# Attention with a token mixer: 128 of 8192 score columns per phase go from ScalarE's exponential to a polynomial on GpSimd and VectorE, with three instead of four buffers for raw weight blocks

## The chip, the cores and the metric

The kernel runs on one NeuronCore of a Trainium2 chip. Its five engines each work through a list of instructions in order and wait for each other on semaphores: TensorE (PE, with its weight loads as PEld), VectorE (DVE), ScalarE (ACT), GpSimd (POOL) and SyncE (SP), which here issues nearly all DMA transfers. The metric is the time of one launch on the device in microseconds (us), lower is better.

## The reference

Two branches work on the same x (2048 tokens, 512 channels, float32) and are mixed row by row with a gate: softmax attention with 32 heads of 16 channels, and a token mixer, that is a layer norm and a two-layer MLP across the 2048 tokens.

```python
g = sigmoid((x * gate_w).sum(-1, keepdims=True))
q, k, v = (x @ wqkv) as 32 heads of 16
a = softmax(q @ k.T * 16**-0.5) @ v @ wo          # per head, 2048 x 2048 scores
b = (w2 . gelu(w1 . layernorm(x).T + b1) + b2).T  # along the tokens, 1792 hidden
out = g * a + (1 - g) * b
```

Everything is wanted in nearly full float32, so the matrix products of the mixer are made in three parts (a high and a low part of each operand, without low times low).

## The kernel before

**The stages.** From 0 to about 123 us the kernel transposes x and makes v, q and k; from 123 to 275 us it makes the first layer of the mixer. The rest, 275 to about 1230 us, is the attention, in 128 *phases* (the loop over `p`, lines 993 to 1156), four to a *group*. A group is two heads and half of the queries. In one phase PE makes 16 score blocks of 128 keys by 512 queries (line 1067), something takes the exponential of each, and PE multiplies them by v in 64 small matmuls (line 963). The second layer of the mixer and the output projections have no time of their own: their matmuls (line 1076, tile `dn`) run beside the score matmuls, on the other half of PE's rows, 12 or 14 in a phase.

**Who makes the exponentials.** The blocks of a phase are numbered 0 to 15. Six of them (`SINGLE`, tile `p`) ACT reads from PSUM one by one, four (`TWO`) in two pairs of 1024 columns (line 1031). The last six (`EVAC` = 1, 3, 5, 8, 14, 15) DVE copies from PSUM to one SBUF tile `pe` of 3072 columns (line 1089); when all six are there ACT makes one exponential of the whole tile in place (line 1102). In ACT's list that big one stands at the end of the phase, behind the six and the two pairs. The results of `pe` are used one phase later: `HELD` lists the three pairs of copied blocks whose product with v heads the next phase's 64 matmuls.

**Order of the work.** The whole attention runs under a manual schedule: each engine's list is the order in which the Python code calls it. At the start of a phase with `ph == 0` the code asks for the next group's q stack (`load_q`, 8 transfers, line 470, tile `qs`); then for each even phase it builds the 14 matmul steps of the mixer that two phases share, and that building calls `load_weight` whenever a step begins a new block of four weight tiles (`fc % 4 == 0`, `second_layer`). After that, still with `ph == 0`, the previous group's result is stored (lines 949 and 951, tiles `ot`, 8 transfers). At `ph == 1` the code asks for the next group's k stack (`load_k`, 6 transfers, line 470, tile `ks`). All of these are on SP's one list. In the last phase of a group (`ph == 3`) matmuls 8 to 21 of the 64 each wait for one of those 14 transfers (`await_loads` in `apply_v`), and the scores of the next group read them.

**The weight blocks.** A block of `w2` (up to four 128x128 tiles) is brought to a raw tile by `load_weight` (line 146, `w_raw`, four buffers), split into a high part by a copy (`w_hi`, line 67) and a low part by a subtraction on GpSimd (`w_lo`, line 68), and is then in the list `ready`. In the attention `split_weight` is called only in the second of two phases (odd `p`), behind everything else of that phase, and only until `ready` holds two blocks. A row tile t of the second layer takes four blocks: two are asked for at the start of its first two phases, one in each of the next two pairs. Between the rows of t = 0 to 7 a late q projection takes one more pair of phases, so those rows start every 8 phases, and later ones every 6.

**GpSimd** has little to do in the attention: `w_lo`, a clearing of the sum tile once a group (line 999), and once a phase a one-element write (`token`, line 1080) that waits for the phase's last `dn` matmul and for which the next phase's first `dn` matmul waits.

Of the kernel before, what the change touches and what calls it, by code (L numbers as in the profile page):

```python
# [9 lines left out]
F32 = mybir.dt.float32  # L10
F32R = mybir.dt.float32r
BF16 = mybir.dt.bfloat16
I32 = mybir.dt.int32
AF = mybir.ActivationFunctionType
ALU = mybir.AluOpType
# [8 lines left out]
P = 128  # L24
# [4 lines left out]
DH = 16  # L29
# [3 lines left out]
NB = 512  # L33
NQ = S // NB
VC = DH + 1
SCALE = DH**-0.5
# [19 lines left out]

LEAST_SUM = 1e-35


@with_exitstack  # L60
def gated_mix(ctx: ExitStack, tc: tile.TileContext, a_x, a_wqkv, a_wo, b_w1, b_b1, b_w2, b_b2, gate_w, out):
    nc = tc.nc
# [15 lines left out]
    const = ctx.enter_context(tc.tile_pool(name="const", bufs=1))  # L78
# [18 lines left out]
    mv = const.tile([P, NS, 2], F32, name="mv")  # L97
    rs = const.tile([P, NS], F32, name="rs")

    const.tile([P, 16], F32, name="pad")  # L100
    upper = ctx.enter_context(tc.tile_pool(name="upper", bufs=1, side="right"))
    upper.tile([P, 56], F32, name="pad_upper")
    v_pool = ctx.enter_context(tc.tile_pool(name="v", bufs=1, reuse_waits="tile"))
# [11 lines left out]
    wk = wk_ctx.enter_context(tc.tile_pool(name="wk", bufs=3, side="right"))  # L115
# [19 lines left out]
    def load_weight():  # L135
        if blocks:
            src = blocks.pop(0)
            raw = wk.tile([P, NB], F32, name="w_raw", bufs=4)
            if len(src.shape) == 2:
                raw = raw[:, : src.shape[1]]  # L140
                dst = raw
            else:
                raw = raw[:, : src.shape[1] * P]
                dst = raw.rearrange("p (k s) -> p k s", s=P)
            with tc.issue_after(x_load.ins):
                nc.sync.dma_start(dst, src)
            loaded.append(raw)
# [30 lines left out]
    with tc.tile_pool(name="vp", bufs=1, side="right") as pool:  # L178
# [143 lines left out]
        y, t, w = (pool.tile([P, NS], F32, name=n) for n in "ytw")  # L322
# [103 lines left out]
    with tc.tile_pool(name="gl", bufs=2, side="right") as gl:  # L426
# [74 lines left out]
        for f0, cs in order.items():  # L501
            n = min(NB, F - f0) // P
# [79 lines left out]
    LAST = NG * PHASES - 1  # L582
# [163 lines left out]
    def invert(half, k, pairs, at):  # L746


        n = pairs * 2
        w = QW // DH  # L750
        t = out_pool.tile([P, w], F32, name="inv")[: n * DH]
        nc.sync.dma_start(t, r_d[half][k][:n].rearrange("r (a b) -> (r a) b", b=w))

        def turn():
            nc.vector.tensor_scalar_max(t, t, LEAST_SUM)
            nc.vector.reciprocal(t, t)

        def put_back():
            nc.sync.dma_start(ri_d[half][k][:n].rearrange("r (a b) -> (r a) b", b=w), t)

        if half and k == ND - 1:
            amid[at + 1] = [(turn,)]
            on_dve(at + 1, put_back)
        else:
            on_dve(at, turn)
            calls.setdefault(at + 1, []).insert(0, (put_back,))
# [110 lines left out]
    for t in range(NS):  # L877
        at = put(second_layer(t), at, [14] * 3)
        if queries:
            b, n = queries.pop(0)  # L880
# [32 lines left out]
    call(p0 + 9, fetch_o, 2, p0 + 13, p0 + 14, p0 + 14)  # L913
    call(LAST, lambda: fetch_o(3, LAST, LAST, LAST, pairs=3))

    token, mark = (out_pool.tile([1, 1], F32, name=name, bufs=1) for name in ("token", "mark"))

    EVAC = 1, 3, 5, 8, 14, 15
    SINGLE = 0, 2, 4, 6, 7, 9
    TWO = (10, 11), (12, 13)  # L920
    TURNS = [(0, 2), (4, 6), (7, 9), *TWO]
    HELD = [(1, 3), (5, 8), (14, 15)]

    def shares(n):

        for one in range(0, BANKS, 2):
            lows = [k for k in range(one)][::2] + [k for k in range(one + 1, BANKS)][::2]
            for third in lows:
                if n in (third, third + 1):
                    first, second = (low for low in lows if low != third)  # L930
                    return [first, first + 1, one, second, second + 1, 2 * third + 1 - n, n]


    def regions():
        return tc.tile_pool(name="ps_s", bufs=1, space=PSUM, reuse_waits="tile")
# [52 lines left out]

    engines = {getattr(mybir.EngineType, name) for name in ("PE", "Activation", "DVE", "Pool", "SP")}
    with tc.manual_schedule(engines=engines):  # L990
        held, fence, turn, spare = [], None, 0, 0
        landed.clear()

        for p in range(LAST + 1):
# [38 lines left out]
                    units[j] = *units[j][:3], pt[:, k - low, :]  # L1033

            pairs_done = []
            evac = evp.tile([P, len(EVAC), NB], F32, name="pe")
            units = {}
            share = shares(spare)
            pool = regions()
# [2 lines left out]
            for n in in_turn:  # L1042
                i, qb = head[n], qbs[n]
                c = at[i][qb]
                at[i][qb] += 1
                if n < TWO[0][0]:
                    if n >= BANKS:
                        ones[share[n - BANKS]] = psum.tile([P, NB], F32, name=f"s{share[n - BANKS]}")
                    s = ones[share[n % BANKS]]
                else:  # L1050
                    if n == TWO[0][0]:
                        pool.__exit__(None, None, None)
                        pool = regions()
                        psum = pool.__enter__()
                        twos = {}
                        for low in range(BANKS):
                            if low == share[2]:
                                av = psum.tile([P, NB], F32, name="av")
                            elif low in (share[0], share[1]):
                                twos[low] = psum.tile([P, NB], F32, name=f"u{low}")  # L1060
                            elif low not in twos:
                                two = psum.tile([P, 2, NB], F32, name=f"t{low}")
                                twos[low], twos[low + 1] = two[:, 0, :], two[:, 1, :]
                                twos[low, low + 1] = two
                    s = twos[share[(n - BANKS) % BANKS]]
                rows_i = slice(i * HALF, i * HALF + ROWS)
                nc.tensor.matmul(  # L1067
                    s,
                    kt[grp][rows_i, c * P : (c + 1) * P],
                    qt[grp][rows_i, qb * NB : (qb + 1) * NB],  # L1070
                    start=True,
                    stop=True,
                )
                if n < n_b:
                    ps, a, b, begin, last, done = beside[n]
                    mm = nc.tensor.matmul(ps, a[half], b[half], start=begin and not second, stop=last and bool(second))  # L1076
                    if n == 0 and fence is not None:
                        tc.add_manual_dep(mm.ins, fence.ins.name, SYNC, reason=REASON)
                    if n == n_b - 1:
                        fence = nc.gpsimd.memset(token, 0.0)  # L1080
                        tc.add_manual_dep(fence.ins, mm.ins.name, SYNC, reason=REASON)
                if n == in_turn[-2]:
                    if n_b and second and beside[-1][-1] in between:
                        between[beside[-1][-1]]()
                    for what, *args in amid.get(p, ()):
                        what(*args)
                if n in EVAC:
                    pt = evac[:, EVAC.index(n), :]
                    nc.vector.tensor_copy(pt, s)  # L1089
                    units[n] = i, c, qb, pt  # L1090
                elif n in SINGLE:
                    pt = ptp.tile([P, NB], F32, name="p1", bufs=len(SINGLE))
                    one = nc.scalar.activation(pt, s, AF.Exp, scale=SCALE)  # L1093
                    if n == SINGLE[-1] and p:
                        tc.add_manual_dep(one.ins, earlier.ins.name, SYNC, reason=EARLY)
                    units[n] = i, c, qb, pt
                else:
                    units[n] = i, c, qb, None
                    if n in (TWO[0][1], TWO[1][1]):
                        exps(n)  # L1100
            for x in ([evac] if p < LAST else [evac[:, :2, :], evac[:, 2:, :]]):
                done = nc.scalar.activation(x, x, AF.Exp, scale=SCALE)  # L1102
            tc.add_manual_dep(done.ins, pairs_done[0].ins.name, SYNC, reason=EARLY)
            evac_done.append(done)
# [206 lines left out]
```

## Time and profile before

| | |
|---|---|
| median of three runs | 1262.76 us (1262.38 to 1263.31) |
| the profiled execution | 1262.86 us, with a span of 1261.1 us from its first to its last instruction |
| granted TensorE clock over the span | 1.000 |
| busy share of the span | PE 99%, ACT 85%, DVE 67%, POOL 16% |
| the attention, from the first phase's scores to the last's | 275.5 to 1222.6 us |
| DMA traffic | 152.31 MB, 121 GB/s on average |

The page of the profile gives the busy time of each engine, the chain of work that ended last, and groups of equal instructions with their count, busy time and mean duration, followed by the idle time in front of them and who ended it. The timeline lists instructions in order of time: start, duration from the start of the first to the end of the last, engine, line, operation, tiles, count, and in brackets the idle time before. Matmuls overlap each other, so PE reads as busy while it is held up for short times. Instructions of ACT and DVE overlap too, by a start before the end of the one in front; what an engine gets done is read from the distance of ends or of starts, not from durations. GpSimd's durations are rough. SPq is SP's own queue: a transfer's row shows when it was issued, not when it landed.

### The profile page before, as it was taken

Reading aid. Unit: us, or ns where it says so; the run is one execution under the profiler, and the core shown is the slowest. Engines: PE = TensorE matmul, PEld = TensorE weight load, DVE = VectorE, ACT = ScalarE, POOL = GpSimd, SP = SyncE. Lnnn points to the kernel's source line nnn. Section 1 sums busy time; section 2 is a strip of 40 time slices with the busy share of each in tenths; the row PEclk is TensorE's granted clock in tenths of the full one; section 3 lists DMA queues with packets and bytes.
Section 4 is the critical chain, followed back from the end, with each engine's and each line's share of the span. In section 5 each row is a group of like instructions: output and inputs, shape, how many; then the busy total and the mean of one; then the engine's idle time right before and its main releaser. Section 6 shows DMA issues by size and latency. Waiting matters only on the chain.

```text
span 1261.1 us, 32707 instructions
## 1 busy us (share of the span) xinstructions
PE 1253.0 (99%) x13342; PEld 827.9 (66%) x13342; DVE 850.8 (67%) x1562; ACT 1068.7 (85%) x1405; POOL 199.2 (16%) x316
## 2 busy tenths in 40 slices
PE   9999999999999999999999999999999999999998
PEld 7888888875666666666666666666666666666656
DVE  5675453178767676667667677776777677678883
ACT  4453343269999999999999999999999999999990
POOL 0220444561011101010110101111111111000000
PEclk9999999999999999999999999999999999999999
DMA  4799443253754443534344433444543443367621
GB/s 130 249 341 330 146 124 108 80 139 109 207 126 102 88 100 83 160 84 97 85 100 94 105 87 79 93 86 81 116 99 77 86 100 60 56 165 174 152 61 70
DMA packets 100555, 152.31 MB, mean 121 GB/s; under 512 B 17109, under 2 KB 56171, under 8 KB 96300
## 3 DMA queue, kind: packets, MB, share of 16 engines
q1 hardware_dynamic: 99820, 149.08, 46.6%
q8 instruction: 107, 1.75, 0.6%
q10 hardware_dynamic: 576, 1.05, 0.2%
q14 instruction: 52, 0.43, 0.1%
HBM read 105.39 MB, written 44.68 MB: 119 GB/s over the span
## 4 chain that ended last, share of the span: by engine, by line
PE 99%; ACT 1%; DVE 0%; issue 0%
PE av L963 32%; PE s L1067 23%; PE acc L424 12%; PE t L1067 9%; PE acc L75 8%; PE t L963 5%; PE u L1067 3%; PE dn L1076 3%; PE pa L1162 2%; PE acc L199 1%; PE acc L268 1%; PE acc L245 0%; ACT p L1093 0%; ACT pe L1102 0%; PE dn L1162 0%; PE pa L1192 0%
## 5 line engine op out<-in xcount | busy, mean ns | idle before, releaser
L1093 ACT ACTIVATE p<-s 128x512 f32<-128x512 f32 x768 | 412.3, 790 | 0.1
L1102 ACT ACTIVATE pe<-pe 128x3072 f32<-128x3072 f32 x129 | 381.8, 2962 | 0.0
L1067 PE MATMUL s<-qs,ks 64*128 64x512 f32 x1280 | 330.0, 400 | 0.6 <-ACT p L1093 0.6
L1089 DVE COPY pe<-s 128x512 f32<-128x512 f32 x512 | 318.1, 683 | 4.8 <-PE s L1067 0.8
L1067 PEld LDWEIGHTS s<-qs,ks 64*128 64x128 f32 x1280 | 225.6, 184 | 95.4 <-issue 45.3
L1031 ACT ACTIVATE p<-t 128x1024 f32<-128x1024 f32 x256 | 278.4, 1265 | 0.0
L963 PE MATMUL av<-p,v 128*32 128x256 f32 x3880 | 227.2, 379 | 0.0
L1089 DVE COPY pe<-u 128x512 f32<-128x512 f32 x256 | 164.8, 686 | 72.1 <-PE u L1067 72.1
L963 PE MATMUL av<-pe,v 128*32 128x256 f32 x3072 | 192.5, 383 | 0.0
L985 DVE TENSOR_TENSOR ot<-av,ot 128x512 f32<-128x512 f32 (+2 forms) x160 | 93.1, 582 | 141.5 <-PE av L963 140.2
L68 POOL TENSOR_TENSOR w_lo<-w_raw,w_hi 128x512 fp32r<-128x512 f32 (+1 forms) x128 | 153.5, 1206 | 194.5 <-ACT w_hi L67 101.8
L1076 PE MATMUL dn<-u_lo,w_hi 64*128 64x512 f32 x448 | 180.8, 404 | 0.0
L1076 PE MATMUL dn<-u_hi,w_hi 64*128 64x512 f32 x448 | 180.7, 403 | 0.0
L963 PEld LDWEIGHTS av<-p,v 128*32 128x32 f32 x3880 | 126.1, 110 | 83.2 <-ACT p L1093 0.2
L1076 PE MATMUL dn<-u_hi,w_lo 64*128 64x512 f32 x448 | 180.7, 403 | 0.0
L1067 PE MATMUL t<-qs,ks 64*128 64x512 f32 x512 | 142.5, 413 | 0.0
L963 PEld LDWEIGHTS av<-pe,v 128*32 128x32 f32 x3072 | 86.8, 109 | 82.1 <-ACT p L1093 37.8
L1080 POOL MEMSET token<- 1x1 f32 x128 | 11.3, 88 | 742.4 <-PE dn L1076 720.5
L67 ACT CAST w_hi<-w_raw 128x512 fp32r<-128x512 f32 (+1 forms) x67 | 38.0, 570 | 80.9 <-PE acc L424 59.4
L1067 PEld LDWEIGHTS t<-qs,ks 64*128 64x128 f32 x512 | 72.9, 184 | 51.2 <-ACT p L1093 49.9
L424 PE MATMUL acc<-h_hi,w_hi 128*128 128x512 f32 x224 | 87.1, 389 | 0.0
L424 PE MATMUL acc<-h_lo,w_hi 128*128 128x512 f32 x224 | 87.1, 389 | 0.0
(171 smaller groups left out, 1615.0 us busy)
## 6 DMA issues: line engine op xcount, KB each, us to landing
w_raw<-in_B_w_dram SPq DMA_DIRECT2D x96, 256.0 KB
ks<-kp SPq DMA_DIRECT2D x192, 128.0 KB
qs<-qp SPq DMA_DIRECT2D x256, 64.0 KB
kp<-pc SPq DMA_DIRECT2D x16, 512.0 KB
qp<-pc SPq DMA_DIRECT2D x8, 768.0 KB
qp<-row SPq DMA_DIRECT2D x24, 256.0 KB
v<-v SPq DMA_DIRECT2D x4, 1088.0 KB
x<-in_A_x_dram SPq DMA_DIRECT2D x16, 256.0 KB
```

What stands on the lines that cost most here:

```text
L67: copy(hi, src)
L68: return sub(lo, src, hi.bitcast(F32), ALU.subtract)
L75: nc.tensor.matmul(ps, a, b, start=start and n == 0, stop=stop and n == last)
L424: nc.tensor.matmul(p, a, b, start=first and k == 0, stop=last and k == 2)
L963: mm = nc.tensor.matmul(av[32 * j : 32 * (j + 1), i * QC : (i + 1) * QC], vb[b][:, v_at : v_at + 32], pt[:, h * QC : (h + 1) * QC], start= ...
L985: latest["add"] = nc.vector.tensor_tensor(x, y, x, ALU.add)
L1031: pairs_done.append(nc.scalar.activation(pt, twos[low, low + 1], AF.Exp, scale=SCALE))
L1067: nc.tensor.matmul(s, kt[grp][rows_i, c * P : (c + 1) * P], qt[grp][rows_i, qb * NB : (qb + 1) * NB], start=True, stop=True,)
L1076: mm = nc.tensor.matmul(ps, a[half], b[half], start=begin and not second, stop=last and bool(second))
L1089: nc.vector.tensor_copy(pt, s)
L1093: one = nc.scalar.activation(pt, s, AF.Exp, scale=SCALE)
L1102: done = nc.scalar.activation(x, x, AF.Exp, scale=SCALE)
```

## The change

It has four parts.

- In phases 0 to 126 the first 128 columns of block 1, the first copied score, are taken out of ACT's big exponential, which shrinks from 3072 to 2944 columns. GpSimd makes 2^y for them: five instructions behind the copy of block 1 (`powers`: scale, round to an integer, fraction, and the exponent's bits), and six behind `token` (`polynomial`). The last two steps of the polynomial are two `scalar_tensor_tensor` of 128 columns on DVE (`product`), placed in the next phase behind the copy of block 8, the fourth copy.
- `HELD` is turned so that the pair (1, 3) is multiplied by v last of the three; a matmul of it now waits for DVE.
- The raw weight blocks have three buffers instead of four.
- GpSimd gets three scratch tiles of 128 columns; `token` and `mark` move to another pool, and `inv` has one buffer.

The core of the diff:

```diff
-            raw = wk.tile([P, NB], F32, name="w_raw", bufs=4)
+            raw = wk.tile([P, NB], F32, name="w_raw", bufs=3)
...
-    HELD = [(1, 3), (5, 8), (14, 15)]
+    HELD = [(5, 8), (14, 15), (1, 3)]
...
+    def powers(raw):
+        by, bt, bg = (evp.tile([P, ON_POOL], F32, name=f"b{x}") for x in "ytg")
+        nc.gpsimd.tensor_scalar(by, raw, SCALE * LOG2E, 0.0, ALU.mult, ALU.add)
+        nc.gpsimd.tensor_scalar(bt, by, 1.0, MAGIC + BIAS, ALU.mult, ALU.add)
+        nc.gpsimd.tensor_scalar(bg, bt, 1.0, -(MAGIC + BIAS), ALU.mult, ALU.add)
+        nc.gpsimd.tensor_tensor(bg, bg, by, ALU.subtract)
+        nc.gpsimd.tensor_scalar(bt.bitcast(I32), bt, 2.0**23, -MAGIC * 2.0**23, ALU.mult, ALU.add)
+        return by, bt, bg
+
+    def polynomial(by, bt, bg):
+        nc.gpsimd.tensor_scalar(by, bg, POWER2[5], POWER2[4], ALU.mult, ALU.add)
+        nc.gpsimd.tensor_tensor(by, by, bg, ALU.mult)
+        for k in (3, 2):
+            nc.gpsimd.tensor_scalar(by, by, 1.0, POWER2[k], ALU.mult, ALU.add)
+            nc.gpsimd.tensor_tensor(by, by, bg, ALU.mult)
+
+    def product(raw, by, bt, bg):
+        nc.vector.scalar_tensor_tensor(by, by, POWER2[1], bg, ALU.add, ALU.mult)
+        nc.vector.scalar_tensor_tensor(raw, by, POWER2[0], bt, ALU.add, ALU.mult)
...
                     if n == n_b - 1:
                         fence = nc.gpsimd.memset(token, 0.0)
                         tc.add_manual_dep(fence.ins, mm.ins.name, SYNC, reason=REASON)
+                        if p < LAST:
+                            polynomial(*begun)
...
                     nc.vector.tensor_copy(pt, s)
+                    if n == EVAC[0] and p < LAST:
+                        begun = powers(pt[:, :ON_POOL])
+                    if n == EVAC[3] and unfinished:
+                        product(*unfinished)
...
-            for x in ([evac] if p < LAST else [evac[:, :2, :], evac[:, 2:, :]]):
+            if p < LAST:
+                unfinished = copies[:, :ON_POOL], *begun
+            for x in ([copies[:, ON_POOL:]] if p < LAST else [copies[:, : 2 * NB], copies[:, 2 * NB :]]):
                 done = nc.scalar.activation(x, x, AF.Exp, scale=SCALE)
```

The added lines move every later line number: 146 becomes 153, 470 becomes 477, 949 and 951 become 975 and 977, 1089 becomes 1118.

**SP at the start of phase 16** (the first phase of group 4; row tile t = 2 begins there). The tiles: `w_raw` the two blocks asked for at once, `qp` a part of the late q projection, `o` and `r` the stores of the previous group, `ks` the next group's k stack. Words in brackets are the semaphores that a row waits for, DMAHW for transfers on the same lane. Before:

```order
L146 DMA w_raw<-in_B_w_dram 128x4x128 [waits DMAHW6_49,Pool_49]
L146 DMA w_raw<-in_B_w_dram 128x4x128 [waits DMAHW7_49,Pool_49]
L631 DMA qp_65<-row 128x512 [waits DMAHW0_49,DVE_49]
L949 DMA o_2590<-ot 16x2x256 [waits DMAHW1_49,DVE_49]
L951 DMA r_2598<-ot 2x1x256 [waits DMAHW2_49]
L949 DMA o_2590<-ot 16x2x256 [waits DMAHW3_49]
L951 DMA r_2598<-ot 2x1x256 [waits DMAHW4_49]
L949 DMA o_2590<-ot 16x2x256 [waits DMAHW5_49,DVE_49]
L951 DMA r_2598<-ot 2x1x256 [waits DMAHW6_49]
L949 DMA o_2590<-ot 16x2x256 [waits DMAHW7_49]
L951 DMA r_2598<-ot 2x1x256 [waits DMAHW0_49]
L470 DMA ks_2582<-kp_86 16x2048 [waits DMAHW1_49]
```

The same place in the changed kernel:

```order
L153 DMA w_raw<-in_B_w_dram 128x4x128 [waits DMAHW6_49,Pool_49]
L153 DMA w_raw<-in_B_w_dram 128x4x128 [waits DMAHW7_49,Pool_49]
L638 DMA qp_65<-row 128x512 [waits DMAHW0_49]
L975 DMA o_2591<-ot 16x2x256 [waits DMAHW1_49]
L977 DMA r_2599<-ot 2x1x256 [waits DMAHW2_49]
L975 DMA o_2591<-ot 16x2x256 [waits DMAHW3_49]
L977 DMA r_2599<-ot 2x1x256 [waits DMAHW4_49]
L975 DMA o_2591<-ot 16x2x256 [waits DMAHW5_49]
L977 DMA r_2599<-ot 2x1x256 [waits DMAHW6_49]
L975 DMA o_2591<-ot 16x2x256 [waits DMAHW7_49]
L977 DMA r_2599<-ot 2x1x256 [waits DMAHW0_49]
L477 DMA ks_2583<-kp_86 16x2048 [waits DMAHW1_49]
```

No transfer moved. But the second `w_raw` now waits for a later GpSimd instruction: with three buffers, block 77 goes where block 74 lay, and block 74 is split at the end of phase 17, not before phase 16. The three waits for DVE below it are gone, because whatever that GpSimd instruction waited for on DVE now covers them.

**DVE in one phase of the attention**, from the third copy on; `pe` is the tile of copied scores, `s` and `u` are score blocks in PSUM. Before:

```order
L1089 COPY pe<-s_4749 128x512 [waits PE_49]
L1089 COPY pe<-s_4780 128x512 [waits PE_49]
L1089 COPY pe<-u_4794 128x512 [waits PE_49]
L1089 COPY pe<-u_4795 128x512 [waits PE_49]
L1111 MEMSET mark 1x1 [waits DVE_49,Activation_49]
```

And in the changed kernel, with `by`, `bg` and `bt` GpSimd's scratch tiles:

```order
L1118 COPY pe<-s_5057 128x512 [waits PE_49]
L957 SCALAR_TENSOR_TENSOR by<-by,bg 128x128 [waits Pool_49]
L958 SCALAR_TENSOR_TENSOR pe<-by,bt 128x128 [waits DVE_49]
L1118 COPY pe<-u_5073 128x512 [waits PE_49]
L1118 COPY pe<-u_5074 128x512 [waits PE_49]
L1146 MEMSET mark 1x1 [waits Activation_49]
```

The two new steps stand between the fourth copy and the two copies of the blocks 14 and 15, and finish the previous phase's 128 columns.

**GpSimd in one phase** had one row before, `token`, or with it the subtractions of a split. Now it has twelve; most wait for the one in front of them:

```order
L942 TENSOR_SCALAR by<-pe 128x128 [waits DVE_49]
L943 TENSOR_SCALAR bt<-by 128x128 [waits Pool_49]
L944 TENSOR_SCALAR bg<-bt 128x128 [waits Pool_49]
L945 TENSOR_TENSOR bg<-bg,by 128x128 [waits Pool_49]
L946 TENSOR_SCALAR bt<-bt 128x128
L1107 MEMSET token 1x1 [waits PE_49]
L950 TENSOR_SCALAR by<-bg 128x128 [waits Pool_49]
L951 TENSOR_TENSOR by<-by,bg 128x128 [waits Pool_49]
L953 TENSOR_SCALAR by<-by 128x128 [waits Pool_49]
L954 TENSOR_TENSOR by<-by,bg 128x128 [waits Pool_49]
L953 TENSOR_SCALAR by<-by 128x128 [waits Pool_49]
L954 TENSOR_TENSOR by<-by,bg 128x128 [waits Pool_49]
```

In an odd phase the subtractions `w_lo` of the split stand behind these twelve; before, they stood behind `token` alone.

More of the change, by code (lines that the diff above doesn't have):

```diff
@@ L57 @@
 LEAST_SUM = 1e-35
+LOG2E = 1.4426950408889634
+MAGIC = 1.5 * 2.0**23
+BIAS = 127.0
+POWER2 = 1.0000001192092896, -0.6931469440460205, 0.24022120237350464, -0.05550713092088699, 0.009675540961325169, -0.001327647129073739
+ON_POOL = 128
 @with_exitstack
@@ L98, in gated_mix @@
     rs = const.tile([P, NS], F32, name="rs")
-    const.tile([P, 16], F32, name="pad")
+    token, mark = (const.tile([1, 1], F32, name=name) for name in ("token", "mark"))
     upper = ctx.enter_context(tc.tile_pool(name="upper", bufs=1, side="right"))
@@ L750, in invert @@
         w = QW // DH
-        t = out_pool.tile([P, w], F32, name="inv")[: n * DH]
+        t = out_pool.tile([P, w], F32, name="inv", bufs=1)[: n * DH]
         nc.sync.dma_start(t, r_d[half][k][:n].rearrange("r (a b) -> (r a) b", b=w))
@@ L914, in gated_mix @@
     call(LAST, lambda: fetch_o(3, LAST, LAST, LAST, pairs=3))
-    token, mark = (out_pool.tile([1, 1], F32, name=name, bufs=1) for name in ("token", "mark"))
     EVAC = 1, 3, 5, 8, 14, 15
@@ L990, in gated_mix @@
     with tc.manual_schedule(engines=engines):
-        held, fence, turn, spare = [], None, 0, 0
+        held, fence, turn, spare, unfinished = [], None, 0, 0, None
         landed.clear()
@@ L1035, in gated_mix @@
             pairs_done = []
-            evac = evp.tile([P, len(EVAC), NB], F32, name="pe")
+            copies = evp.tile([P, len(EVAC) * NB], F32, name="pe")
+            evac = copies.rearrange("p (n x) -> p n x", x=NB)
             units = {}
```

## The prediction, made before the changed kernel had run

> **What bounds the kernel now.** I read the page first:
>
> ```profile
> PE 1253.0 (99%) x13342; PEld 827.9 (66%) x13342; DVE 850.8 (67%) x1562; ACT 1068.7 (85%) x1405; POOL 199.2 (16%) x316
> PE 99%; ACT 1%; DVE 0%; issue 0%
> ```
>
> The chain of work that ended last is PE nearly throughout. But overlapping matmuls hide short waits, and ACT's 85% includes the first 275 us, where it has little to do. So I read ACT's timeline over two phases in the middle:
>
> ```profile
> 697.15 3.00 ACT L1102 ACTIVATE pe<-pe 128x3072 f32<-128x3072 f32 x1
> 699.85 3.24 ACT L1093 ACTIVATE p<-s 128x512 f32<-128x512 f32 x6
> 702.73 2.20 ACT L1031 ACTIVATE p<-t 128x1024 f32<-128x1024 f32 x2
> 704.57 3.01 ACT L1102 ACTIVATE pe<-pe 128x3072 f32<-128x3072 f32 x1
> ...
> 711.98 3.01 ACT L1102 ACTIVATE pe<-pe 128x3072 f32<-128x3072 f32 x1
> ```
>
> The big exponentials start 7.42 us apart, each instruction starts before the one in front has ended, and no row has idle time. ACT is full. For PE, the chain in order of time gives the starts of the 64 matmuls with v in several phases:
>
> ```profile
> 421.29 3.66 PE av L963 x64
> ...
> 703.15 3.66 PE av L963 x64
> 710.57 3.66 PE av L963 x64
> ...
> 1118.87 3.59 PE av L963 x64
> 1126.19 3.60 PE av L963 x64
> 1133.51 3.60 PE av L963 x64
> ```
>
> In the middle they are 7.42 us apart, as on ACT. Late, behind a stall that let ACT clear its queue, they are 7.32 us apart twice: that is what PE needs when ACT doesn't hold it. That ACT does hold it otherwise is one row of the waits:
>
> ```profile
> PEld t L1067 <- ACT p L1093: 49.9, 243, 0.3
> ```
>
> So ACT sets 7.42 us a phase and PE is 0.10 behind it.
>
> **The exponential.** The last phase has the big one in two pieces, and they give the price of a column:
>
> ```profile
> L1102 ACT ACTIVATE pe<-pe 128x2048 f32<-128x2048 f32 x1 | 2.1, 2057 | 0.0
> L1102 ACT ACTIVATE pe<-pe 128x1024 f32<-128x1024 f32 x1 | 1.2, 1202 | 0.0
> ```
>
> (2057 - 1202)/1024 = 0.835 ns. 128 columns less are 0.107 us, so ACT's phase becomes 7.42 - 0.11 = 7.31, and PE's 7.32 is next. The gain is at most 0.10 us x 123 phases (the first four have other work) = 12 us.
>
> **GpSimd's eleven steps.** None of this form is in the trace. Rows around them:
>
> ```profile
> L68 POOL TENSOR_TENSOR w_lo<-w_raw,w_hi 128x512 fp32r<-128x512 f32 x96 | 127.2, 1327 | 182.5 <-ACT w_hi L67 92.2 <-DVE w_hi L67 90.2
> L68 POOL TENSOR_TENSOR w_lo<-w_raw,w_hi 128x256 fp32r<-128x256 f32 x32 | 27.0, 843 | 12.1 <-ACT w_hi L67 9.5 <-DVE w_hi L67 1.7 <-DVE u_lo L446 0.6
> L1080 POOL MEMSET token<- 1x1 f32 x128 | 11.3, 88 | 742.4 <-PE dn L1076 720.5 <-PE t L1067 21.9
> masks.py:199 POOL TENSOR_SCALAR_AFFINE_SELECT ident<-ident 128x128 f32<-128x128 f32 x1 | 0.3, 292 | 0.0
> ```
>
> A one-input step of this size: 0.29 us. A two-input step, extrapolated from 512 and 256 columns: 843 - (1327 - 843)/2 = 601 ns, an upper bound since these means hold waits. Seven and four of them are 4.4 us. GpSimd idles 742/128 = 5.8 us a phase, so it is not filled; the six steps behind `token` take 3 x 0.29 + 3 x 0.60 = 2.7 us. [...]
>
> **DVE's two steps.** Their place in the phase:
>
> ```profile
> 700.08 2.48 DVE L1089 COPY pe<-s 128x512 f32<-128x512 f32 x4
> 703.18 1.29 DVE L1089 COPY pe<-u 128x512 f32<-128x512 f32 x2 [0.62 <-PE u L1067]
> ...
> 706.87 0.69 DVE L985 TENSOR_TENSOR ot<-av,ot 128x512 f32<-128x512 f32 x1 [1.85 <-PE av L963]
> ```
>
> A two-input step takes, by columns:
>
> ```profile
> L985 DVE TENSOR_TENSOR ot<-av,ot 128x512 f32<-128x512 f32 x11 | 7.5, 684 | 4.4 <-PE av L963 4.4
> L985 DVE TENSOR_TENSOR ot<-av,ot 128x256 f32<-128x256 f32 x4 | 1.7, 419 | 0.3 <-PE av L963 0.3
> ```
>
> 128 columns: 419 - (684 - 419)/2 = 286 ns. Two are 0.57 us and just fit the 0.62 us in which DVE waits for block 14 anyway. If they run longer, the copies of 14 and 15 and with them ACT's big exponential come later; that one now starts 702.73 + 2.20 - 704.57 = 0.36 us before its predecessor ends, so a few tenths more are covered as well. I take 0.08 of the 0.10 us a phase, with 0 and 0.10 as ends: 123 x 0.08 = 9.8 us gained.
>
> **PE's new wait** (pair (1, 3), for DVE) comes after the fourth-copy position, which the scores of block 15 wait for already: nothing.
>
> **The three buffers in the first layer.** There SP asks for a wide block each 2.72 us:
>
> ```profile
> 190.38 0.35 SPq L146 DMA_DIRECT2D w_raw<-in_B_w_dram  x1
> ...
> 193.09 0.35 SPq L146 DMA_DIRECT2D w_raw<-in_B_w_dram  x1
> ```
>
> With three buffers a transfer has three such distances less the split of its predecessor, 1.3 us for the subtraction and, estimated at half of that, 0.7 for the copy: 8.2 - 2.0 = 6.2 us. The narrow blocks have about half of it, 3 us. I count 0, with a us in all as the other end.
>
> **The three buffers in the attention.** This is the term that I think decides. SP in phases 16 and 17 before, and the split that the second `w_raw` will wait for:
>
> ```profile
> 397.70 0.94 SPq L146 DMA_DIRECT2D w_raw<-in_B_w_dram  x2
> 401.00 0.36 SPq L631 DMA_DIRECT2D qp<-row  x1
> 401.46 0.67 SPq L949 DMA_DIRECT2D o<-ot  x1
> ...
> 405.97 2.71 SPq L470 DMA_DIRECT2D ks<-kp  x6
> ...
> 406.35 0.09 POOL L1080 MEMSET token<- 1x1 f32 x1 [7.33 <-PE dn L1076]
> 408.22 1.99 POOL L68 TENSOR_TENSOR w_lo<-w_raw,w_hi 128x512 fp32r<-128x512 f32 x2 [1.78 <-DVE w_hi L67]
> ```
>
> At the start of phase 16 `ready` holds blocks 72 and 73, and 74 and 75 are raw. Blocks 76 and 77 are asked for at once. With four buffers they go where 72 and 73 lay, both split. With three, 76 takes 73's place and 77 takes 74's, which is split at the end of phase 17. So SP stands at block 77 from 398.2 to the end of that subtraction: 408.22 + 1.29 = 409.5 at best (the pair takes 1.99, its half-size second 0.7), and 406.44 + 2.7 + 1.29 = 410.4 when it comes behind the six new steps. That SP does stop at such a transfer, its list being in order, is in SP's waits:
>
> ```profile
> SPq L146 <- POOL w_lo L68: 112.8, 65, 4.2
> ```
>
> At most 4.2 us so far; now some 12. Behind it: the rest of the `w_raw` (0.5), `qp` (0.4), the eight stores (405.97 - 401.46 = 4.5), then `ks`. The first `ks` is issued at 410.4 + 5.4 = 415.8 instead of 405.97. When have all six landed? Busy share of the DMA engines:
>
> ```profile
> 414.00:415.00 1.00, 1.00 (x24) 0.57 (x24) 1.00 (x2) 1.00 (x2) 0.00 (x0) 1.00 0.39 104
> 415.00:416.00 1.00, 1.00 (x24) 0.62 (x20) 0.20 (x2) 1.00 (x2) 0.00 (x0) 1.00 0.00 1
> ```
>
> By 415.0, that is up to 9.0 us behind the first issue. So now 415.8 + 9.0 = 424.8. They are wanted by matmul 21 of phase 19, 421.29 + 21 x 3.66/64 = 422.5. Before there were 7.5 us to spare; now PE waits 2.3 us. Ends: 1.4 with the early release, 0.6 less if the transfers drain faster without the `w_raw` beside them, 0.7 more if GpSimd is slower: 0.8 to 3.0. I take 2.2. ACT has nothing to do meanwhile, so it is added to the time.
>
> How often: in groups at whose first phase a row tile starts, p = 8, 16, ... 64, then 76, 88, 100: 11 times. (Rows that start in the third phase of a group, 70, 82 and 94, hold back only transfers with a group's time to spare.) 11 x 2.2 = 24.2 us, ends 9 and 33.
>
> **Sum**, against the profiled execution of 1262.86 us (0.1 above the median): 1262.9 - 9.8 + 24.2 = 1277 us. About 0.2%, 2.5 us, is what a measurement can tell from no change.
>
> **Rivals.**
>
> *The k stack comes in time* (faster; chance 0.14). Place: `ks` in the last phase of those 11 groups. If SP got to it 2.3 us sooner, say because the transfers drain in 7 us and not 9 and GpSimd's steps are short, nothing waits and the full gain stands: 1263 - 11 = 1252 us. For it: the 9.0 us is one reading. Against: even the early release leaves 0.8 us.
>
> *They cancel* (within 0.2%; 0.10): 11 waits of 0.8 to 1.0 against a gain of 10 to 12 give 1261 to 1264.
>
> *DVE and GpSimd get in each other's way* (slower still; 0.16). One place shows it already:
>
> ```profile
> 304.64 1.67 DVE L68 TENSOR_TENSOR u_lo<-row,u_hi 128x512 fp32r<-128x512 f32 x1
> 304.35 1.41 POOL L68 TENSOR_TENSOR w_lo<-w_raw,w_hi 128x512 fp32r<-128x512 f32 x1 [1.76 <-DVE w_hi L67]
> ```
>
> Both read two SBUF tiles; DVE's ended 0.55 us after GpSimd's, and took 1.67 us where its kind takes 0.7. The two new DVE steps read two SBUF tiles each and run while GpSimd ends `powers` and starts `polynomial`. Each could wait out one step, 0.3 to 0.6 us; with both held the copies come 0.6 to 1.2 us late, 0.3 is covered, and about half the rest returns as a longer phase. That costs the gain and some 0.1 us a phase more: 1263 + 24 + 12 = 1299 us. [...] Against: copies from PSUM aren't touched, and half of the time GpSimd waits for `token` there.
>
> **Chances.** Forecast 0.60 with its own range of 1266 to 1290; the rivals 0.14, 0.10, 0.16. Slower 0.76, same 0.10, faster 0.14. The range over the cases, leaving out the full gain and the worst contention: 1260 to 1294.
>
> **What would show it.** ACT's big exponential at about 2.9 us and phases 7.32 to 7.35 us apart within a group; SP's wait for `w_lo` at line 153 with about 12 us as its longest; PE idle, or its matmuls with v stretched, for 2 us in phases 11, 19, 27. Wrong if `ks` is issued as early as before, or if phases without such a load are 7.42 us or longer: then the gain, not the wait, was misjudged.

## The result, and the profile after

The changed kernel takes 1284.37 us (median of six runs, 1282.83 to 1285.91) against 1262.74 for the kernel before: a ratio of 1.0169, 95% interval 1.0156 to 1.0182. It is slower by 21.6 us. The profiled execution took 1282.83 us, with a span of 1281.0; before it was 1262.86 and 1261.1.

The same lines as before, from the page of the changed kernel (busy time of the engines, and the chain that ended last by engine):

```profile
PE 1258.8 (98%) x13342; PEld 858.1 (67%) x13342; DVE 926.2 (72%) x1816; ACT 1060.0 (83%) x1405; POOL 716.1 (56%) x1713
PE 82%; SPq 6%; DMA 5%; POOL 3%; ACT 1%; issue 1%; DVE 1%; POOLq 0%; ACTq 0%
```

The chain was PE for 99% of the span; now 14% of it is SP's queue, DMA transfers and GpSimd. PE itself has the same work (13342 matmuls). Between those places the phases got shorter. ACT's timeline (start, duration, engine, line, tiles, count) and PE's matmuls with v from the chain, both in undisturbed phases:

```profile
712.40 2.82 ACT L1137 ACTIVATE pe<-pe 128x2944 f32<-128x2944 f32 x1
...
719.71 2.81 ACT L1137 ACTIVATE pe<-pe 128x2944 f32<-128x2944 f32 x1
```

```profile
318.56 3.59 PE av L989 x64
325.87 3.60 PE av L989 x64
333.21 3.59 PE av L989 x64
```

The distance from phase to phase is 7.31 to 7.34 us where it was 7.42. So the forecast gain is there, and the 21.6 us are losses beside it. The first of them is where the prediction put it. SP's timeline in phases 16 and 17 (phase 16 now starts at 397.06):

```profile
400.27 12.88 SPq L153 DMA_DIRECT2D w_raw<-in_B_w_dram  x2
413.20 0.50 SPq L638 DMA_DIRECT2D qp<-row  x1
...
417.97 4.08 SPq L477 DMA_DIRECT2D ks<-kp  x6
```

The pair of `w_raw` took 0.94 us and now takes 12.88, and the first `ks` goes out 20.9 us after the phase's start, where it was 10.8 (405.97 - 395.21). GpSimd's list at the end of phase 17 shows what SP waits for, and PE's, in phase 19, what it does for want of the k stack:

```profile
410.64 0.30 POOL L953 TENSOR_SCALAR by<-by 128x128 f32<-128x128 f32 x1
411.03 0.46 POOL L954 TENSOR_TENSOR by<-by,bg 128x128 f32<-128x128 f32 x1
411.44 1.98 POOL L75 TENSOR_TENSOR w_lo<-w_raw,w_hi 128x512 fp32r<-128x512 f32 x2
```

```profile
423.19 1.50 PE L989 MATMUL av<-pe,v 128*32 128x256 f32 x24
424.51 0.61 PE L989 MATMUL av<-p,v 128*32 128x256 f32 x6
425.42 1.26 PE L989 MATMUL av<-p,v 128*32 128x256 f32 x4 [0.30 <-DMA ks<-kp]
426.87 1.93 PE L989 MATMUL av<-p,v 128*32 128x256 f32 x30 [0.19 <-DMA ks<-kp]
```

PE stops ahead of its 31st and again ahead of its 35th matmul with v for a part of the k stack; phase 19 takes 9.26 us.

The largest single loss is one that the prediction doesn't have, in phases 78 and 79. SP's timeline, and DVE's:

```profile
853.31 12.51 SPq L153 DMA_DIRECT2D w_raw<-in_B_w_dram  x2
...
870.16 2.94 SPq L477 DMA_DIRECT2D ks<-kp  x6
873.14 0.42 SPq L702 DMA_DIRECT2D row<-in_A_wo_dram  x1
```

```profile
879.26 0.43 DVE L74 CAST big<-row 128x512 fp32r<-128x512 f32 x1 [9.37 <-DMA row<-in_A_wo_dram]
879.72 0.69 DVE L75 TENSOR_TENSOR big<-row,big 128x512 fp32r<-128x512 f32 x1
880.33 0.68 DVE L1011 TENSOR_TENSOR ot<-av,ot 128x512 f32<-128x512 f32 x1
```

Behind `ks` on SP's list stands a row of `wo`. DVE is to split it at the end of phase 78 and stands still for 9.37 us until it has landed; the sum and the copies of phase 79 are behind it in DVE's list, and PE stops for want of them. Phase 79 takes 16.27 us. Before, the same row was issued at 854.13 and split at 860.20.

Not all of that is waiting. PE's rows around the stop, and one of the view by stretches of time, in which the third number from the end is the granted clock:

```profile
873.40 0.39 PE L1094 MATMUL s<-qs,ks 64*128 64x512 f32 x1
...
881.07 0.79 PE L1094 MATMUL s<-qs,ks 64*128 64x512 f32 x1 [7.27 <-DVE ot L1011]
...
882.94 0.62 PE L1094 MATMUL t<-qs,ks 64*128 64x512 f32 x1
```

```profile
882.00:884.00 2.00, 2.00 (x12) 1.54 (x10) 1.97 (x5) 1.58 (x3) 1.32 (x4) 0.50 0.00 0
```

While PE stands, the clock that it is granted falls from 1.00 to 0.50 (at 877.46) and comes back at 884.29, 3.2 us after PE has started again. Until then PE's score matmuls are 0.43 us apart where 0.23 is usual. Of the 8.9 us that phase 79 is too long, 7.4 are the wait and 1.5 the low clock behind it.

The third loss is DVE's. In the phase before each of eight row tiles (phase 15 here), DVE also brings a late q projection out of the PSUM tile `dn`:

```profile
392.90 0.38 DVE L957 SCALAR_TENSOR_TENSOR by<-by,bg 128x128 f32<-128x128 f32 x1
393.32 0.38 DVE L958 SCALAR_TENSOR_TENSOR pe<-by,bt 128x128 f32<-128x128 f32 x1
393.62 0.68 DVE L623 CAST row<-dn 128x512 fp32r<-128x512 f32 x1
394.22 1.27 DVE L1118 COPY pe<-u 128x512 f32<-128x512 f32 x2
395.42 0.67 DVE L628 TENSOR_TENSOR row<-dn,row 128x512 fp32r<-128x512 f32 x1
396.01 0.73 DVE L629 TENSOR_SCALAR row<-dn,most 128x512 f32<-128x512 f32 x1
396.67 0.67 DVE L630 TENSOR_REDUCE z<-dn 128x1 f32<-128x512 f32 x1
```

No row has idle time: DVE is full, and its last read of `dn` ends at 397.34, 0.28 us after phase 16 has begun at 397.06. The new `dn` matmuls of phase 16 start at 397.50 only. Before, without the two steps in front, that read ended 0.44 us ahead of the phase (394.77 against 395.21).

The two traces set side by side, by the distances between the first score matmuls of successive phases (the sum is that of the spans, 19.9 us):

| place | us |
|---|---|
| 108 phases from 4 to 111, each 0.097 shorter where nothing waits | -10.4 |
| ten waits for the k stack, phases 11, 19, 27, 35, 43, 51, 59, 67, 91, 103 (1.2 to 1.9 each) | +14.8 |
| the wait for the row of `wo` and the low clock behind it, phase 79 | +8.9 |
| eight phases (8, 16, ... 64) that start late on `dn`, 0.43 each | +3.4 |
| phases 36 and 69, each for another reason | +0.5 |
| the first layer and phases 0 to 3 | +1.3 |
| phases 112 to 126, and what follows | +1.3 |

Ahead of phase 36 the reason is one more transfer on SP's list: DVE waits 1.35 us for a piece of `inv`. Phase 69 comes up again with the rival of contention below.

### The profile page after: what moved, and what is told of

The parts are those of the page before. It is cut to its first block, busy times and chain, and to the rows that moved or that the text cites. A ratio compares the mean times of both kernels' runs of the same rounds, so it can differ in the third digit from the quotient of the medians.

```text
span 1281.0 us, 34192 instructions
## 1 busy us (share of the span) xinstructions
PE 1258.8 (98%) x13342; PEld 858.1 (67%) x13342; DVE 926.2 (72%) x1816; ACT 1060.0 (83%) x1405; POOL 716.1 (56%) x1713
## 4 chain that ended last, share of the span: by engine, by line
PE 82%; SPq 6%; DMA 5%; POOL 3%; ACT 1%; issue 1%; DVE 1%; POOLq 0%; ACTq 0%
PE av L989 23%; PE s L1094 17%; PE acc L431 12%; PE acc L82 8%; PE t L1094 6%; PE t L989 5%; PE dn L1103 5%; DMA ks<-kp 5%; PE u L1094 2%; SPq L977 2%; SPq L477 2%; PE pa L1197 2%; SPq L975 1%; POOL w_lo L75 1%; POOL by L954 1%
## 5 line engine op out<-in xcount | busy, mean ns | idle before, releaser
L1126 ACT ACTIVATE p<-s 128x512 f32<-128x512 f32 x768 | 392.2, 633 | 21.8 <-PE dn L1103 18.6
L1137 ACT ACTIVATE pe<-pe 128x2944 f32<-128x2944 f32 x129 | 350.0, 2715 | 5.1 <-DVE pe L1118 4.9
L1057 ACT ACTIVATE p<-t 128x1024 f32<-128x1024 f32 x256 | 258.6, 1110 | 0.3 <-PE t L1094 0.3
L989 PE MATMUL av<-p,v 128*32 128x256 f32 x3880 | 236.7, 379 | 5.3 <-DMA ks<-kp 5.3
L942 POOL TENSOR_SCALAR by<-pe 128x128 f32<-128x128 f32 x127 | 37.9, 298 | 224.2 <-DVE pe L1118 223.4
L954 POOL TENSOR_TENSOR by<-by,bg 128x128 f32<-128x128 f32 x254 | 136.7, 538 | 21.2
L1094 PE MATMUL t<-qs,ks 64*128 64x512 f32 x512 | 137.3, 402 | 0.0
L1094 PEld LDWEIGHTS t<-qs,ks 64*128 64x128 f32 x512 | 81.2, 185 | 34.6 <-ACT p L1126 22.9
L953 POOL TENSOR_SCALAR by<-by 128x128 f32<-128x128 f32 x254 | 82.8, 326 | 22.2
```

What stands on the lines that cost most here:

```text
L954: nc.gpsimd.tensor_tensor(by, by, bg, ALU.mult)
L989: mm = nc.tensor.matmul(av[32 * j : 32 * (j + 1), i * QC : (i + 1) * QC], vb[b][:, v_at : v_at + 32], pt[:, h * QC : (h + 1) * QC], start= ...
L1057: pairs_done.append(nc.scalar.activation(pt, twos[low, low + 1], AF.Exp, scale=SCALE))
L1094: nc.tensor.matmul(s, kt[grp][rows_i, c * P : (c + 1) * P], qt[grp][rows_i, qb * NB : (qb + 1) * NB], start=True, stop=True,)
```

## The experiments

Beside each of the three groups of runs the kernel before took 1263.02, 1262.85 and 1262.90 us (medians).

**Three buffers alone** (e1): the kernel before with one edit.

```diff
-            raw = wk.tile([P, NB], F32, name="w_raw", bufs=4)
+            raw = wk.tile([P, NB], F32, name="w_raw", bufs=3)
```

> The kernel before with three raw weight buffers and nothing else changed. Theory (the loss is SP standing at the second w_raw until GpSimd's split, and what stands behind it on SP's list coming late): without the six polynomial steps the split ends about 1.4 us earlier after the start of its pair of phases (14.3 instead of 15.7 us), so the ten waits for the k stack of 1.2 to 1.9 us shrink to 0 to 0.5 us, 1.4 us in all; the wait for the row of wo shrinks from 8.9 to 7.5 us; the first layer gives 1.5 us: 1262.8 + 1.4 + 7.5 + 1.5 = 1273 us, phases of 7.42 us. Rival A (three buffers cost the same whatever GpSimd does beside them): 1262.8 + 14.9 + 8.9 + 1.5 = 1288 us. Rival B (the loss comes from the new steps on DVE and GpSimd): 1263 to 1265 us.

Measured: 1275.03 us, ratio 1.0094 (1.0077 to 1.0111). SP's waits, first in this kernel, then in the changed one (in total, times, longest):

```profile
SPq L146 <- POOL w_lo L68: 281.4, 80, 13.7
```

```profile
SPq L153 <- POOL w_lo L75: 287.1, 79, 14.4
```

The three buffers alone make SP stand. But the split ends sooner, and of the ten waits for the k stack 3.3 us are left by the phases' distances (1.4 were expected), about half of them in two phases (8.26 and 8.33 us). Phase 79 is 9.2 us too long (16.60 us), not the 7.5 expected. The wait did shrink: PE stands 6.25 us there, and 7.27 in the changed kernel. But the clock is at 0.50 from 870.26 to 880.50, and PE, which starts again at 874.33, has 6.2 us of it instead of 3.2. Rival A, 1288, and rival B, 1265, are both off by more than 9 us. So the buffers alone cost 12 us; the rest needs GpSimd's new steps as well.

**The transfer asked for later** (e2): the changed kernel, but `load_weight` is put off while three raw blocks are unsplit, and made up for behind the split.

```diff
+    def ask(new=True):
+        if new:
+            owed.append(1)
+        while owed and len(loaded) < 3:
+            owed.pop()
+            load_weight()
...
-                load_weight()
+                ask()
...
                     if len(ready) < 2:
                         split_weight(nc.vector.tensor_copy)
+                ask(False)
```

> The changed kernel, but a w_raw transfer that would find no free buffer is asked for only after the split at the end of the odd phase, behind the k stack in SP's list. Theory: the ten waits for the k stack (14.9 us) and the one for the row of wo (8.9 us) go, the gain per phase stays: 1284.4 - 23.8 = 1260.5 us, from 1259 to 1262. Rival B (the loss comes from DVE and GpSimd getting in each other's way): 1280 us or more.

Measured: 1259.17 us, ratio 0.997 (0.996 to 0.998). SP's timeline in phases 16 and 17:

```profile
398.31 0.39 SPq L153 DMA_DIRECT2D w_raw<-in_B_w_dram  x1
401.25 0.36 SPq L647 DMA_DIRECT2D qp<-row  x1
...
406.10 2.71 SPq L486 DMA_DIRECT2D ks<-kp  x6
...
410.82 1.08 SPq L153 DMA_DIRECT2D w_raw<-in_B_w_dram  x2
```

With the same number of buffers and every step of the exponential as in the changed kernel, a later place in SP's list for the transfers that would find no buffer takes 25.2 us away. `ks` goes out 11.0 us after the phase's start again; all ten waits and the stop in phase 79 (7.32 us now) are gone.

**The split ahead of the polynomial** (e3): in odd phases `polynomial(*begun)` is called behind the two `split_weight` instead of behind `token`.

> The changed kernel with GpSimd's subtractions w_lo ahead of the six polynomial steps in odd phases. Theory: the split ends 1.24 us earlier, so of the ten waits (1.2 to 1.9 us each, 14.9 in all) 2.6 us are left and of the wait for the row of wo 7.7 of 8.9: 1284.4 - 12.3 - 1.2 = 1271 us, up to 1274 if the polynomial, now 2 us later, holds DVE's two steps and the copies behind them. Rival A (the six steps ahead of the split don't matter, three buffers alone do): 1284 us.

Measured: 1271.99 us, ratio 1.0072 (1.0055 to 1.0088). GpSimd's timeline:

```profile
406.43 0.09 POOL L1107 MEMSET token<- 1x1 f32 x1 [0.18 <-PE dn L1103]
408.35 1.98 POOL L75 TENSOR_TENSOR w_lo<-w_raw,w_hi 128x512 fp32r<-128x512 f32 x2 [1.83 <-DVE w_hi L74]
410.42 0.30 POOL L950 TENSOR_SCALAR by<-bg 128x128 f32<-128x128 f32 x1
```

The split now waits for DVE and not for the polynomial; it begins 1.92 us behind `token`, where it was 3.03 in the changed kernel (411.44 - 408.41). That 1.1 us counts in every group: the ten waits fall from 14.8 to 5.1 us, and the time by 12.4. Phase 79 gains only 0.4 us (15.91) of the 1.2 expected. So the six steps do matter, and rival A falls.

**The row of `wo` asked for earlier** (e4): `load_wo` one phase earlier, ahead of the `w_raw` pair, its split where it was.

```diff
-                    call(2 * at + 5 + 4 * k, load_wo, k, 2 * at + 5 + 4 * k)
+                    call(2 * at + 4 + 4 * k, load_wo, k, 2 * at + 5 + 4 * k)
```

> The changed kernel with each row of wo asked for one phase earlier, ahead of the w_raw transfers in SP's list; all else the same. Theory: the stop of 8.9 us in phase 79 goes, and the k stack of that group, which it hid, takes its 1.4 us: 1284.4 - 8.9 + 1.4 = 1277 us. Rival (DVE's stop there has another cause than the row's place in SP's list): 1284 us.

Measured: 1275.98 us, ratio 1.0102 (1.0085 to 1.0119). Phase 79 takes 8.00 us instead of 16.27: the row's stop is gone, and what is left, 0.68 us, is the wait for the k stack that it hid. The ten other waits, which this edit leaves alone, sum to 17.2 us in this trace, where they were 14.8 in the changed kernel's: their sum differs by some 2 us from one execution to another.

**Without DVE's two steps** (e5): the kernel of e2 with `product` left out.

> The kernel with the late w_raw request (1259.2 us), with DVE's two new steps left out (the 128 columns stay unexponentiated, all else as there). Theory: in most phases the two steps lie in DVE's wait for block 14 and cost nothing, so phases stay 7.32 us; but in eight phases (7, 15, ... 63) DVE also handles a late q projection and has no room, and the next phase begins 0.43 us late on the PSUM tile dn; those eight 0.43 us go, and about 1 us in the last fifteen phases: 1259.2 - 3.4 - 1 = 1255 us. Rival (the two steps and GpSimd's get in each other's way in every phase): phases shorter than 7.32 us everywhere, 1250 us or less. Rival (they cost nothing at all): 1259 us.

Measured: 1260.98 us, ratio 0.9985 (0.9975 to 0.9994), 1.8 us slower than with the two steps. The eight late phases are gone as expected (7.38 us instead of 7.75). The last phases, from 112 on, are as long as they were, which was not expected. And nearly everywhere three of four phases take 7.38 to 7.40 us, and only each group's second one 7.31 or 7.32. DVE's rows at the start of such a long phase:

```profile
942.01 0.69 DVE L1020 TENSOR_TENSOR ot<-av,ot 128x512 f32<-128x512 f32 x1 [0.98 <-PE av L998]
942.72 2.48 DVE L1127 COPY pe<-s 128x512 f32<-128x512 f32 x4
```

The first copy begins 0.71 us behind the sum ahead of it. In the list of DVE's instructions that copy has two semaphores to wait for, PE's and GpSimd's, in all but the second phase of a group:

```
L1020 TENSOR_TENSOR ot<-av,ot 128x512 [waits PE_49]
L1127 COPY pe<-s_9534 128x512 [waits PE_49,Pool_49]
L1127 COPY pe<-s_9535 128x512 [waits PE_49]
```

It overwrites a tile that GpSimd read two phases earlier. With the two steps in place, their own wait for GpSimd covers that one. That the second wait makes the copy late was a new theory, so it got a run of its own.

**The wait put back without the work** (e9): as e5, with a one-element copy in the place of the two steps.

```diff
                     if n == EVAC[3] and unfinished:
-                        product(*unfinished)
+                        nc.vector.tensor_copy(mark, unfinished[1][:1, :1])
```

> As the kernel without DVE's two steps (1261.0 us), but at their place DVE copies one element of GpSimd's scratch tile, which waits for GpSimd there (the 128 columns stay unexponentiated). Theory (without the two steps, in three of four phases the first copy of scores has to wait for GpSimd besides PE, long after GpSimd is done, and that second wait alone costs 0.065 us a phase): the wait goes back to a place with room, phases are 7.32 us again, 1261.0 - 0.065 x 81 = 1255.7 us. Rival (the two steps themselves shorten a phase in some other way): 1261 us.

Measured: 1254.63 us, ratio 0.9932 (0.9916 to 0.9947): an instruction more, 6.3 us less. The same two rows:

```profile
952.36 0.69 DVE L1020 TENSOR_TENSOR ot<-av,ot 128x512 f32<-128x512 f32 x1 [2.04 <-PE av L998]
952.99 2.48 DVE L1127 COPY pe<-s 128x512 f32<-128x512 f32 x4
```

The copy begins 0.63 us behind the sum, and the phases are 7.32 us nearly throughout.

A second semaphore by itself is not what costs, though. In 42 phases of the changed kernel the same copy waits for two as well, PE's and DVE's own, and begins 0.62 to 0.64 us behind the sum, no later than where it waits for one. Phase 18 is such a phase:

```profile
412.27 0.69 DVE L1011 TENSOR_TENSOR ot<-av,ot 128x512 f32<-128x512 f32 x1 [1.56 <-PE av L989]
412.90 1.29 DVE L1118 COPY pe<-s 128x512 f32<-128x512 f32 x2
```

In the traces each of these copies with two waits has a semaphore instruction of 0.02 us ahead of it, which takes one of them over. In the changed kernel it takes DVE's, long reached, and runs right behind the start of the sum, at 412.28. In e5 it takes PE's, which is the late one: PE's signal comes at 942.63, the semaphore instruction runs at 942.66 and the copy at 942.72. In e9 the copy itself waits for PE: signal 952.97, copy 952.99. So what costs is one more instruction between the late signal and the copy.

Against e2, 4.5 us are what the two DVE steps cost, 3.4 of it in the eight phases.

**A shorter exponential** (e6): the kernel of e2 with `copies[:, 2 * ON_POOL :]` as ACT's operand.

> The kernel with the late w_raw request, with ACT's big exponential cut by a further 128 columns to 2816 (these 128 columns stay unexponentiated; no step is added for them). Theory: PE needs 7.32 us a phase and is the bound, so the phases stay 7.32 us: 1259 us. Rival (ACT still sets the phase at 7.31): another 0.1 us over about 100 phases, 1249 us.

Measured: 1257.55 us, ratio 0.9959 (0.9943 to 0.9974). PE's chain in three phases:

```profile
700.89 3.59 PE av L998 x64
708.20 3.59 PE av L998 x64
715.52 3.59 PE av L998 x64
```

7.31 and 7.32 us, with ACT relieved by another 0.1. PE is the bound now. The 1.6 us less come from places that DVE or ACT sets, as the eight late phases (7.65 instead of 7.75).

**DVE's two steps doubled** (e7): two more `scalar_tensor_tensor` of 128 columns on the scratch tile behind the two.

> The kernel with the late w_raw request, with DVE's two steps doubled to four (two more steps of 128 columns on the scratch tiles, 0.57 us). Theory: the two fill DVE's 0.62 us of waiting; the further 0.57 us make the copies of blocks 14 and 15 come 0.5 to 0.6 us later, about half of which returns as a longer phase beyond what is covered: 0.1 to 0.2 us a phase, 1259 + 12 to 25 = 1271 to 1284 us. Rival (ACT now has slack enough to cover it): 1259 to 1263 us.

Measured: 1299.98 us, ratio 1.0296 (1.0280 to 1.0311), 41 us more than e2, beyond the range given. DVE's groups of the four steps in the stretch from 840 to 1080 us (count, busy time, mean ns):

```profile
L969 DVE SCALAR_TENSOR_TENSOR by<-by,bg 128x128 f32<-128x128 f32 x32 | 13.1, 410 | 1.1
L966 DVE SCALAR_TENSOR_TENSOR by<-by,bg 128x128 f32<-128x128 f32 x32 | 11.3, 355 | 0.0
L968 DVE SCALAR_TENSOR_TENSOR by<-by,bg 128x128 f32<-128x128 f32 x32 | 9.5, 298 | 1.1
L967 DVE SCALAR_TENSOR_TENSOR pe<-by,bt 128x128 f32<-128x128 f32 x32 | 9.3, 292 | 1.1
```

The further two take 0.71 us, not 0.57, and nothing of it is covered: in this stretch phases of 7.32 and of 7.96 us take turns, 0.32 on average. That about half of DVE's delay returns as a longer phase holds; that ACT's slack takes the first tenths off it doesn't. DVE's wait was filled by the change to the brim.

**The share left out where DVE has no room** (e8): the kernel of e2 with

```diff
+    def shared(p):
+        return p < 112 and not (p < 64 and p % 8 == 6)
```

in the place of `p < LAST`, ACT making all 3072 columns elsewhere.

> The kernel with the late w_raw request, with GpSimd's share left out where DVE has no room for the two steps: in the phases 6, 14, ... 62 and from 112 on ACT makes all 3072 columns. Theory: the eight waits of 0.43 us become 0.10 us of ACT's longer exponential, and the last phases take what they took before: 1259.2 - 2.6 - 1.2 = 1255.4 us. Rival (those waits aren't the two steps'): 1259 to 1260 us.

Measured: 1254.27 us, ratio 0.993 (0.9916 to 0.9943). The phases 8, 16, ... 64 take 7.31 to 7.33 us.

**Four buffers back** (e10): the changed kernel with `bufs=4` for `w_raw` and `bufs=1` for GpSimd's three scratch tiles, which makes the room.

> The changed kernel with four raw weight buffers as before the change; the room comes from GpSimd's scratch tiles, which have one buffer each and not two, so GpSimd starts a phase's five steps only when DVE's two of the phase before are done, about 2.3 us later. Theory: SP no longer stands at the second w_raw, the ten waits for the k stack (14.9 us), the one for the row of wo (8.9) and the first layer's 1.5 us go: 1284.4 - 25.3 = 1259 us; the later GpSimd steps still end before the next phase's two on DVE. Rival A (single scratch tiles bind the chain of GpSimd and DVE): 1265 us or more. Rival B (the buffers aren't the cause): 1284 us.

Measured: 1257.23 us, ratio 0.9954 (0.9939 to 0.997). SP's wait:

```profile
SPq L153 <- POOL w_lo L75: 146.0, 76, 4.2
```

Its longest is 4.2 us, as in the kernel before the change, and phase 4 begins at 305.8 us instead of 307.4: the first layer's loss is gone too.

**Both** (e11): e10's buffers with e8's choice of phases.

> Four raw buffers and single scratch tiles, with GpSimd's share left out in the phases 6, 14, ... 62 and from 112 on, as in the run that did so with three raw buffers (1254.3 us). Theory: that time less what three buffers cost in the first layer and the first phase, 1.5 to 2 us: 1252.5 us. Rival (that run's first phase was long for another reason): 1254 us.

Measured: 1253.39 us, ratio 0.9925 (0.9911 to 0.9938), the fastest of all: 9.5 us below the kernel before. Some 0.6 of the missing 0.9 us lies in phases 90 and 102, 7.60 and 7.68 us long, as in e10 (7.60 both) and unlike e8 (7.31 and 7.32). With single scratch tiles GpSimd's steps and the split behind them come later there, and in phase 102 one of DVE's two steps takes 0.82 us beside the subtraction. So the single tiles are the likely cause; no run tests it.

## Why the prediction came out as it did

The direction, the mechanism and the place were right as far as they went: the gain in each phase, SP standing at the second `w_raw`, PE short of the k stack in the last phase of the groups named. That the sum, +14.1 us against +19.9 for the profiled executions, is nearer than its terms is luck: one was too large by 9 us, and some 15 us were left out.

- **The gain.** Taken as 9.8 us with 0.08 a phase; it is 0.097, the full distance from ACT's 7.42 to PE's 7.32, and e6 shows that PE sets the rest.
- **GpSimd's steps.** One-input steps take 0.30 us as taken (0.29), two-input ones 0.46 (0.60 was the upper bound), and the six behind `token` 2.9 us (from 408.58 to 411.49 in phase 17) where 2.7 was taken, since each begins some 0.08 us behind the end of the one ahead. The subtraction of 512 columns takes 1.29 us (median), 0.83 more for 384 more columns or 2.2 ns for each; by that some 0.18 us of the 0.46 don't go by columns, an estimate from the two.
- **SP's stand** was to end at 410.4, 15.2 us behind the phase's start; it was 15.7. First `ks` at 20.6, measured 20.9; all landed 9.0 behind it, measured 8.9. e2 and e10, which take this away, bring back 25.2 and 27.1 us with what it drags along; e10's figure includes the first layer's loss.
- **The step that failed by size** is "They are wanted by matmul 21 of phase 19". The last part of the k stack is waited for ahead of the 35th of the 64 matmuls, as PE's rows above show: the program's matmuls 4 to 17 wait (it has 32, and each is two in the trace), not 8 to 21 of 64 as the description had it. 14 matmuls later are 0.8 us, and 2.2 - 0.8 = 1.4 is close to the ten waits (1.48 on average). Ten and not eleven, since the one in phase 79 was hidden behind a greater one.
- **The step that was missing** is the rest of SP's list. What the prediction put behind the stop (the rest of the `w_raw`, `qp`, the eight stores, then `ks`) is true and stops one entry short: the row of `wo` behind `ks` has DVE waiting for it, 8.9 us with the low clock, more than half of what all ten k stacks cost. e4 shows it by itself.
- **DVE's two steps** "just fit the 0.62 us in which DVE waits" is right for most phases; they take 0.39 and 0.30 us on average. But the wait isn't there in every phase: in eight of them a read of `dn` filled it before. That cost 3.4 us, and e8 gets most of it back.
- **Three buffers in the first layer** were counted 0 with a us as the other end; it was 1.3 (ACT's split waits 1.17 us for a transfer ahead of phase 0), and 2.1 in e1.
- **The rival of contention** (1299 us) falls with e2 in the size that it was given. That a 128-column step of DVE waits out a whole step of GpSimd's, as its sum has it, is shown by no run; what they show is a smaller delay, as in these rows of e2:

```profile
943.48 0.49 DVE L966 SCALAR_TENSOR_TENSOR by<-by,bg 128x128 f32<-128x128 f32 x1
```

```profile
943.36 0.46 POOL L954 TENSOR_TENSOR bg<-bg,by 128x128 f32<-128x128 f32 x1
```

DVE's step begins while GpSimd's runs (to 943.82), both with two SBUF inputs, and takes 0.49 us where its kind takes 0.28 with nothing of GpSimd's beside it (at 1241.30 in the changed kernel). It ends 0.15 us behind GpSimd's, though, and not a whole step behind. That is 0.2 us at a time, 0.1 on average, and not the 0.3 to 0.6 for each of the two that the rival put in. DVE's copies from PSUM, which the prediction takes to be untouched, show no such delay: those of `s` take 683 ns on average in both kernels, those of `u` 680 after and 686 before, with GpSimd busy for 56% of the span and for 16%.

Contention is left as the likely reason for a few long phases. Phases 69, 115, 119 and 123 take 7.57, 7.54, 7.50 and 7.72 us in the changed kernel, and nearly the same in e5 and e9, so it isn't DVE's two new steps. From 112 on they are 7.32 to 7.34 in e8, where GpSimd has no share. In the rows ahead of these phases DVE's other steps run beside GpSimd's polynomial and take longer: ahead of phase 123 a cast (`v<-o_sum`) takes 0.95 us, and 0.69 in e8; ahead of phase 69 a step of 32 columns takes 0.29 us, and 0.17 before the change. For phase 69 no run tests it.

## What to carry to other kernels

Taking a buffer away is a change to the queue that fills it: find which release each transfer now waits for, and follow the queue behind it to its end, since the costliest victim may be the last and not the first. A change on another engine that delays that release (here six short steps ahead of a subtraction) makes it worse, and the two don't add up: the buffers alone cost 12 us, the new steps with four buffers gained 5.7, and both together lost 21.6. Where room on an engine is found in an average or in one phase, look for the phases in which it is already used.

## What the runs showed of the hardware that was not expected

Where the first copy of scores has two semaphores to wait for, it mattered which of them the semaphore instruction ahead of it takes over. Between the two rows of e5 there is one of 0.02 us at 942.66, and in e9 there is none. In e5, where it holds the late wait, it makes three of four phases 7.38 us instead of 7.32, and a one-element copy that takes the other wait over at a place with room (e9) makes the kernel 6.3 us faster. In 42 phases of the changed kernel, where it holds the wait that is long over, it costs nothing: the copy begins 0.62 to 0.64 us behind the sum. Leaving work out cost time here (e5 takes 1.8 us more than e2), and an experiment that leaves work out should be read phase by phase before its time is believed.

A long stop of PE cost more than the stop here. In the three traces in which PE stands for 6 to 7 us in phase 79, its granted clock falls to 0.50 and is back 3.2 us after the restart in the changed kernel, 6.2 in e1 and 4.7 in e3. In e4, which takes that stop away and keeps the short ones, it is 1.00 until the kernel's end. So a stop that is 1 us shorter (6.25 us in e1, 7.27 in the changed kernel) did not give a phase that is shorter: e1's phase 79 is the longer one, 16.60 us against 16.27.
